# An mLSTM attention fused with a bilinear MLP: zero products ahead of the first transposes, a tile of their own for the gates, and another order of transfers and of the opening

## The chip, the cores and the metric

The kernel runs on one core of one Trainium2 chip. A core has the engines PE (TensorE, the matrix products), DVE (VectorE), ACT (ScalarE), POOL (GpSimd) and SP (SyncE, which here issues every DMA). The metric is device microseconds of one execution; lower is better. Before the change the median of three runs is 582.19 us (581.82 to 582.39).

## The reference, cut to what matters

For 4 batches and 8 heads a matrix memory C and a vector n run over 768 steps; the gated read-out y of all heads goes through a bilinear MLP. There is no softmax.

```python
for t in range(S):
    m_new  = np.maximum(f_gate[:, :, t] + m, i_gate[:, :, t])
    f_stab = np.exp(f_gate[:, :, t] + m - m_new)
    i_stab = np.exp(i_gate[:, :, t] - m_new)
    m = m_new
    C = f_stab * C + i_stab * einsum('bhd,bhe->bhde', vt, kt)
    n = f_stab * n + i_stab * kt
    h_tilde = einsum('bhde,bhe->bhd', C, qt)
    denom = np.maximum(np.abs(einsum('bhd,bhd->bh', n, qt)), 1.0)
    y[:, :, t] = sigmoid(o_gate[:, :, t]) * h_tilde / denom
x = y.transpose(0, 2, 1, 3).reshape(B * S, H * D)      # 3072 x 320
out = (x @ w_a) * (x @ w_b) @ w_out                    # 320 x 1536, 1536 x 320
```

The weights arrive in float64, everything else in float32.

## The kernel before, in words

**Attention.** The 768 steps are cut into 6 pieces of 128; a piece of one batch is a *chunk*, so there are 24, chunk n being piece n // 4 of batch n % 4. For a chunk the kernel transposes q and k on PE (`begin_a`, tile `pT`, copied to `T`), makes the table of decays (`begin_e`, product `pE` and an exponential into `gbc`), multiplies k by q (`pS`) and that by the table, multiplies by v (`begin_c`, `pV`), adds what the state of earlier pieces gives (`pI`), divides and gates it (`stage_f`, tiles `den`, `osig`), and turns it into the MLP's two operands `xh` and `xl` (`stage_d`, `pX`), a high and a low part. `weigh` makes `vw` = v times a column of weights on POOL; `stage_u` multiplies it by k into the state (`pU`, `cst`). From chunk 4 on the table comes from DRAM instead: the gates' sums are written to `g_dram`, `load_g` spreads them over 128 partitions into `gbc`, POOL masks them (line L405), and ACT takes eight exponentials (L412). From chunk 6 on q and k are split into three bf16 parts and turned by DMA transposes.

**MLP.** Nine *blocks* of 2 or 3 chunks go through `moe_block`. For each of 12 slices ff of the hidden width, `up(ff)` makes two sums `pu` of eight products each (the letter h or l of a weight is its high or low part), ACT copies the first, DVE multiplies by the second (`g`), and two slices later `down(ff)` adds three products per chunk into `pd`.

**Weights.** float64 cannot be computed with, so each piece of weights, a *stage* x from 0 to 31, is fetched raw (`fetch`) and converted by `high` (ACT), `low` and `join` (DVE, L347 and L352), `lead_part` (ACT, a copy that rounds, L365) and `low_part` (DVE, the rest, L371). Stages 0 to 4 serve slices 0 to 2 of the up-projection (0, 2 and 4 its first sum; 1, 3 and 4 its second), 5 to 7 the first three slices of the down-projection, 8 to 12 the next three slices up, and so on. `ready` tells how far the conversion stands, and `need` forces it.

**The order.** PE, ACT, DVE and SP work through fixed rows, in an order that a scheduler makes of the order of the code, of priorities and of `tc.issue_after`, which holds an instruction behind another one. What is written in the opening (after `manual_schedule`) is two chunks and stages 0 to 4 by hand. After it, `moe_block` yields after each product, and between products the generator `att` (the attention of later chunks) and `conv` (the weights) get their turns: `conv` at every sixth product.

**Rooms.** The gates' tables (`room`: f, i, m, `tab`, `gb`) sit in the slots s24 to s28, which are those of the raw weights of stages 24 to 28. So those can be fetched only when the gates are done, and `weights` fetches stage x + 16 as it converts stage x (`AHEAD`).

Of the kernel before, what the change touches and what calls it, by code (L numbers as in the profile page):

```python
# [8 lines left out]
F32 = mybir.dt.float32  # L9
BF16 = mybir.dt.bfloat16  # L10
# [10 lines left out]
def kernel(  # L21
# [116 lines left out]
    def load_qk(n, parts=(0, 1)):  # L138
        c, b = chunks[n]
        for j in parts:  # L140
            x = (q, k)[j]
            issued["qk"[j], n] = nc.sync.dma_start(  # L142
                nat(n)[0][:, j, :, 0:D], x[b, :, c * P:(c + 1) * P, :].rearrange("h t d -> t h d")
            ).ins

    def load_v(n):
        c, b = chunks[n]
        nc.sync.dma_start(
            nat(n)[1][:, :, 0:D], v[b, :, c * P:(c + 1) * P, :].rearrange("h t d -> t h d")
        )  # L150

    def load(n):
        load_qk(n)
        load_v(n)

    def fetch_o(c, b):
        if c not in osig:
# [25 lines left out]

        return x.bitcast(BF16).rearrange("p h (d w) -> p h d w", w=2)[:, :, :, 1]

    room = [rpool.tile([P, S], F32, tag=f"s{24 + j}", name=f"g_{n}") for j, n in enumerate(("f", "i", "m", "tab", "gb"))]
    gf, gi, gm = (x[0:BH] for x in room[0:3])
    tab = room[3][0:3 * BH].rearrange("p (c t) -> p c t", c=NC)
    gb3 = room[4][0:BH].rearrange("p (j w t) -> p j w t", j=3, w=2)

    def fetch_gates(cols):
        for t, x in ((gf, f_gate), (gi, i_gate)):
# [1 line left out]

    def first_gates():
        f, i, m = (x[:, 0:P] for x in (gf, gi, gm))
        g = gb3[:, 0]
        nc.vector.tensor_tensor_scan(m, f, i, -1e30, op0=ALU.add, op1=ALU.max)
        nc.vector.memset(f[:, 0:1], 0.0)
        nc.vector.tensor_tensor(f[:, 1:], f[:, 1:], m[:, 0:P - 1], op=ALU.add)  # L200
        nc.vector.tensor_tensor(f[:, 1:], f[:, 1:], m[:, 1:], op=ALU.subtract)
        nc.vector.tensor_tensor_scan(
            g[:, 0], one.broadcast_to([BH, P]), f, 0.0, op0=ALU.mult, op1=ALU.add
        )
        nc.vector.tensor_tensor(g[:, 1], i, m, op=ALU.subtract)
        nc.vector.tensor_tensor(g[:, 1], g[:, 1], g[:, 0], op=ALU.subtract)
        for j in range(3):
            x = gb3[:, j]
            (nc.scalar.copy if j < 2 else nc.vector.tensor_copy)(stk[j * BH:(j + 1) * BH], top(x))
            if j < 2:  # L210
                nc.vector.tensor_tensor(gb3[:, j + 1], x, top(x), op=ALU.subtract)

    def later_gates():
        f, i, m = (x[:, P:] for x in (gf, gi, gm))
# [6 lines left out]
        nc.vector.tensor_tensor(i, i, m, op=ALU.subtract)  # L221
        yield
        with tc.issue_after(start["act"]):
            nc.scalar.copy(G[:, 0], gb3[:, 0, 0])
            nc.scalar.copy(tab[BH:2 * BH, 0], gb3[:, 0, 1])
        for c in range(1, NC):
            nc.vector.tensor_tensor_scan(
                G[:, c], one.broadcast_to([BH, P]), gf[:, c * P:(c + 1) * P], 0.0,
# [78 lines left out]

    ready = [0]
    NF0 = 5
    AHEAD = 16  # L310

    def need(x):

# [355 lines left out]
    def moe_block(kb):  # L669
# [26 lines left out]
        def up(ff):  # L696
# [5 lines left out]
            for j in range(2):  # L702
                terms = []
                for kt in range(2):
                    h, l = w_up(ff, kt, j)
                    terms += [(h, xh[:, kt, :]), (h, xl[:, kt, :]), (l, xh[:, kt, :])]

                h = w_up(ff, 2, j)
                terms += [(h, xh[:, 2, :]), (h, xl[:, 2, :])]
                for x, (a, r) in enumerate(terms):  # L710
                    nc.tensor.matmul(  # L711
                        acc[j], a, r, start=(x == 0), stop=(x == len(terms) - 1),
                    )
                    yield
                if j == 0:
                    g = mpool.tile([P, NTB], F32, tag="acp", name=f"g{kb}_{ff}")[:, 0:NT]
                    (nc.vector.tensor_copy if kb > 0 and ff in [1, 2] else nc.scalar.copy)(g, acc[0])  # L717
# [35 lines left out]
    def begin_a(n):  # L753
# [6 lines left out]
        for j in range(2):  # L760
# [9 lines left out]
            for x in range(HH):  # L770
                after["t"] = nc.tensor.transpose(
                    pt[:, x], nat(n)[0][:, j, 2 * x:2 * x + 2, :].rearrange("t h d -> t (h d)"), ident
                ).ins
            (nc.vector.tensor_copy if n > 0 and j == 1 else nc.scalar.copy)(t, pt)
# [87 lines left out]
    with tc.manual_schedule(engines={mybir.EngineType[x] for x in ("PE", "Activation", "DVE", "SP")}):  # L862
        fetch_gates(slice(0, P))
        load_qk(0)
        fetch(0)
        load_qk(1)
        fetch(2)
        load_v(0)
        fetch(4)
        load_v(1)  # L870
        fetch_o(0, 0)
        fetch(1)
        fetch_o(0, 1)
# [19 lines left out]
        first_gates()  # L893
        run(A[0], 2)
        high(0)
        low(0)
        join(0)
        lead_part(0)
        run(E[0], 2)
        low_part(0)  # L900
        run(S_[0])
        run(A[1])
        high(2)
        low(2)
        join(2)
        run(S_[0])
        run(A[1])
        run(S_[0])
        run(E[1], 2)
        run(S_[1])  # L910
        lead_part(2)
        low_part(2)
        run(V[0], 2)
        squash(0, 0, 1)
        run(S_[1], 2)
        high(4)
        low(4)
        join(4)
        run(V[0])
        run(V[1], 2)  # L920
        run(F[0])
        lead_part(4)
# [89 lines left out]
```

## Time and profile before

| | before |
|---|---|
| median of three runs | 582.19 us |
| the profiled execution, its own time | 586.26 us |
| its span, first to last instruction | 584.5 us |
| PE busy | 543.7 us (93%) |
| DVE busy | 414.7 us (71%) |
| ACT busy | 220.0 us (38%) |
| POOL busy | 128.3 us (22%) |
| mean granted TensorE clock | 0.95 |

Busy time is the time in which an engine had at least one instruction under way. A row of the timeline has start and length in us, the engine (SPq is the issue of a DMA on SP), the line of the kernel, what is written from what, and in brackets how long the engine had been idle and what ended that. The granted clock is the share of the full TensorE clock that the chip's throttle allowed; the profile knows it from its first record, 8.9 us into the span, and shows 1.00 ahead of that.

### The profile page before, as it was taken

Reading aid. Unit: us, or ns where it says so; the run is one execution under the profiler, and the core shown is the slowest. Engines: PE = TensorE matmul, PEld = TensorE weight load, DVE = VectorE, ACT = ScalarE, POOL = GpSimd, SP = SyncE. Lnnn points to the kernel's source line nnn. Section 1 sums busy time; section 2 is a strip of 40 time slices with the busy share of each in tenths; the row PEclk is TensorE's granted clock in tenths of the full one; section 3 lists DMA queues with packets and bytes.
Section 4 is the critical chain, followed back from the end, with each engine's and each line's share of the span. In section 5 each row is a group of like instructions: output and inputs, shape, how many; then the busy total and the mean of one; then the engine's idle time right before and its main releaser. Section 6 shows DMA issues by size and latency. Waiting matters only on the chain.

```text
span 584.5 us, 12445 instructions
## 1 busy us (share of the span) xinstructions
PE 543.7 (93%) x4800; PEld 519.7 (89%) x4800; DVE 414.7 (71%) x947; ACT 220.0 (38%) x547; POOL 128.3 (22%) x181
## 2 busy tenths in 40 slices
PE   5697899999899989999799998998999999999997
PEld 5585799999799889999799898898999999999997
DVE  5689976457879767788739877678949774954332
ACT  5375854444323623323613323344413621411101
POOL 2002424444413230332103330312303201100000
PEclk9587669989999989999899999999999999999999
DMA  9995913494866774467634677566625832500000
GB/s 174 296 297 138 199 32 89 87 165 86 154 146 116 135 150 89 110 148 114 139 88 93 148 151 119 126 117 136 133 72 121 152 43 71 75 2 24 0 1 34
DMA packets 198678, 66.75 MB, mean 114 GB/s; under 512 B 184252, under 2 KB 191900, under 8 KB 198620
## 3 DMA queue, kind: packets, MB, share of 16 engines
q1 hardware_dynamic: 198620, 65.98, 54.3%
q8 instruction: 37, 0.61, 0.5%
q14 instruction: 21, 0.17, 0.1%
HBM read 41.11 MB, written 5.97 MB: 81 GB/s over the span
## 4 chain that ended last, share of the span: by engine, by line
PE 57%; DMA 13%; DVE 12%; SPq 9%; ACT 4%; issue 3%; POOL 0%; ACTq 0%; DVEq 0%
PE pu L711 32%; PE pd L684 14%; DMA T<-qks 4%; SPq L329 3%; PE pV L519 2%; DMA raw<-in_moe_w_out_dram 2%; DMA gbc<-g_dram 2%; DMA osig<-in_o_gate_dram 2%; SPq L159 2%; DVE gbc L472 2%; PE pX L618 2%; PE pV L836 1%; DMA c_dram<-cb 1%; SPq L142 1%; PE pS L784 1%
## 5 line engine op out<-in xcount | busy, mean ns | idle before, releaser
L711 PE MATMUL pu<-xh,w 128*128 128x384 f32 (+1 forms) x1080 | 285.0, 332 | 5.5 <-ACT g L717 1.5
L711 PE MATMUL pu<-xl,w 128*128 128x384 f32 (+1 forms) x648 | 211.5, 328 | 0.0
L711 PEld LDWEIGHTS pu<-xh,w 128*128 128x128 f32 x1080 | 197.5, 196 | 10.2 <-ACT g L717 2.8
L684 PE MATMUL pd<-w,gh 128*128 128x320 f32 x576 | 131.2, 315 | 2.0 <-ACT gh L720 1.6
L711 PEld LDWEIGHTS pu<-xl,w 128*128 128x128 f32 x648 | 126.5, 196 | 0.3
L718 DVE TENSOR_TENSOR g<-pu,g 128x384 f32<-128x384 f32 (+1 forms) x108 | 54.7, 507 | 76.9 <-PE pu L711 38.0
L684 PEld LDWEIGHTS pd<-w,gh 128*128 128x128 f32 x576 | 98.2, 191 | 3.0 <-ACT gh L720 2.1
L684 PE MATMUL pd<-w,gl 128*128 128x320 f32 x288 | 88.2, 316 | 0.1
L717 ACT COPY g<-pu 128x384 f32<-128x384 f32 (+1 forms) x92 | 40.3, 438 | 87.8 <-PE pu L711 77.2
L454 POOL TENSOR_TENSOR vr<-va 128x336 f32<-128x336 f32 x18 | 14.0, 779 | 212.7 <-PE pV L519 212.7
L684 PEld LDWEIGHTS pd<-w,gl 128*128 128x128 f32 x288 | 54.0, 190 | 0.9 <-DVE gl L722 0.3
L412 ACT ACTIVATE gbc<-gbc,gtab 128x128 f32<-128x128 f32 x160 | 49.3, 389 | 11.9 <-POOL gbc L405 9.6
L722 DVE TENSOR_TENSOR gl<-g,gh 128x384 fp32r<-128x384 f32 (+1 forms) x92 | 51.9, 564 | 1.9
L430 ACT CAST qks<-qk 128x320 bf16<-128x320 f32 x36 | 16.5, 457 | 80.4 <-DMA T<-qks 65.6
L720 DVE CAST gh<-g 128x384 fp32r<-128x384 f32 (+1 forms) x96 | 37.5, 390 | 1.6
L441 DVE COPY qks<-qks 128x320 bf16<-128x320 bf16 x36 | 10.4, 293 | 32.9 <-ACT qks L430 29.1
L405 POOL TENSOR_SCALAR_AFFINE_SELECT gbc<-gbc 128x1024 f32<-128x1024 f32 x20 | 25.5, 1277 | 21.1 <-DMA gbc<-g_dram 21.1
L595 POOL TENSOR_TENSOR osig<-osig,den 128x320 f32<-128x320 f32 x22 | 18.0, 819 | 48.9 <-DVE den L590 37.5
L519 PE MATMUL pV<-va,pb 128*128 128x42 bf16 x288 | 25.0, 182 | 0.6 <-DVE pb L478 0.6
L722 POOL TENSOR_TENSOR gl<-g,gh 128x256 fp32r<-128x256 f32 x16 | 13.0, 811 | 57.0 <-ACT gh L720 54.0
L519 PEld LDWEIGHTS <-pb 128*128 128x128 bf16 x576 | 23.0, 96 | 2.7 <-issue 0.9
L476 DVE TENSOR_TENSOR gbc<-gbc,pb 128x512 f32<-128x512 f32 x36 | 24.1, 683 | 1.0 <-ACT pb L474 0.8
(125 smaller groups left out, 807.3 us busy)
## 6 DMA issues: line engine op xcount, KB each, us to landing
gbc<-g_dram SPq DMA_DIRECT2D x20, 512.0 KB
qk<-in_q_dram SPq DMA_DIRECT2D x24, 160.0 KB
qk<-in_k_dram SPq DMA_DIRECT2D x24, 160.0 KB
va<-in_v_dram SPq DMA_DIRECT2D x24, 160.0 KB
osig<-in_o_gate_dram SPq DMA_DIRECT2D x24, 160.0 KB
raw<-in_moe_w_out_dram SPq DMA_DIRECT2D x12, 320.0 KB
out_dram<-o SPq DMA_DIRECT2D x24, 160.0 KB
raw<-in_moe_w_a_dram SPq DMA_DIRECT2D x8, 384.0 KB
```

The source lines that it names most:

```text
L329: raw_in = nc.sync.dma_start(raw[r0:r0 + a.shape[0]], a).ins
L405: nc.gpsimd.affine_select(E, E, pattern=[[0, H], [1, P]], compare_op=ALU.is_ge, fill=-1e30, base=0, channel_multiplier=-1,)
L412: nc.scalar.activation(E[:, h], E[:, h], AF.Exp, bias=beta[:, h:h + 1])
L476: nc.vector.tensor_tensor(E, E, pb[:, 0], op=ALU.subtract)
L519: nc.tensor.matmul(pv[:, h], pb[i][:, h % HH, :], vb[j][:, h], start=(x == 0), stop=(x == len(terms) - 1),)
L595: (nc.vector if n < NS else nc.gpsimd).tensor_tensor(yv, yv, den.unsqueeze(2).broadcast_to([P, H, D]), op=ALU.mult)
L684: nc.tensor.matmul(pd[t][:, 0:DM], a[:, cols], w, start=(ff == 0 and first), stop=(ff == NF - 1 and last),)
L711: nc.tensor.matmul(acc[j], a, r, start=(x == 0), stop=(x == len(terms) - 1),)
L717: (nc.vector.tensor_copy if kb > 0 and ff in [1, 2] else nc.scalar.copy)(g, acc[0])
L718: nc.vector.tensor_tensor(g, acc[1], g, op=ALU.mult)
L720: (nc.vector.tensor_copy if kb > 0 else nc.scalar.copy)(gh, g)
L722: (nc.gpsimd if kb * 12 + ff < 16 else nc.vector).tensor_tensor(gl, g, gh.bitcast(F32), op=ALU.subtract)
```

## The change

- Ten products of a zeroed tile (`idle`) go to a bank of their own (`warm`) at the head of PE's rows.
- The gates get tiles of their own (`gfim`, `g_tab`, `g_b`). So all stages are fetched in one run at the opening, `AHEAD` is gone, and the loads of chunk 3 and later, the write of `g_dram` and the first loads of `gbc` are held behind the last of the weights (`issued["w"]`).
- The attention's generator is held behind the first product of the first up-projection (`start["pe"]`), and so are chunk 2's transposes.
- The load of chunk 3 moves behind the state update of chunk 0, the long scan of the gates ahead of chunk 2's transposes, v of chunks 0 and 1 ahead by a stage, the second transposed copy of chunk 0 from ACT to DVE; the opening is written in another order; the conversion gets its turn at every fourth product of the first block.

```diff
     def load(n):
-        load_qk(n)
-        load_v(n)
+        with tc.issue_after(issued.get(("v", n - 1), issued["w"])):
+            load_qk(n)
+            load_v(n)
...
-    room = [rpool.tile([P, S], F32, tag=f"s{24 + j}", name=f"g_{n}") for j, n in enumerate(("f", "i", "m", "tab", "gb"))]
...
+    gfim = wpool.tile([3 * BH, S], F32, name="gfim")
+    gf, gi, gm = (gfim[j * BH:(j + 1) * BH] for j in range(3))
+    tab = wpool.tile([3 * BH, NC, P], F32, name="g_tab")
+    gbt = wpool.tile([3 * BH, 2, P], F32, name="g_b")
...
-        nc.sync.dma_start(g_dram.rearrange("c g t -> g c t"), G)
+        with tc.issue_after(issued["w"]):
+            nc.sync.dma_start(g_dram.rearrange("c g t -> g c t"), G)
...
     def weights():
         for x in range(NF0, len(stages) + 1):
-            fetch(x + AHEAD)
...
         for n in range(NS, NCH):
             if n + 1 < NCH:
-                with tc.issue_after(issued["w"]):
-                    load(n + 1)
+                if n > NS:
+                    with tc.issue_after(issued["w"]):
+                        load(n + 1)
...
-            (nc.vector.tensor_copy if n > 0 and j == 1 else nc.scalar.copy)(t, pt)
+            (nc.vector.tensor_copy if j == 1 else nc.scalar.copy)(t, pt)
...
-        for x in range(16, NF0 + AHEAD):
+        for x in range(16, 24):
             fetch(x)
+        for x in range(24, len(stages)):
+            fetch(x)
+
+        idle = apool.tile([P, H * DV], F32, tag="vr", name="idle").bitcast(BF16)[:, 0:512]
+        nc.vector.memset(idle, 0.0)
+        warm = ps_dn.tile([P, 512], F32, tag="pd2", name="warm")
+        for _ in range(WARM):
+            nc.tensor.matmul(warm, idle[:, 0:P], idle, start=True, stop=True)
...
     def rest():
+        gates = later_gates()
+        for _ in range(2):
+            next(gates)
+            yield
         yield from begin_a(NS)
         yield from begin_e(NS)
-        yield from later_gates()
+        yield from gates
         for n in range(NS):
             weigh(n)
             yield from stage_u(n)
+            if n == 0:
+                with tc.issue_after(issued["w"]):
+                    load(NS + 1)
...
-            if x % 6 == 0:
+            if x % (4 if kb == 0 else 6) == 0:
                 next(conv, None)
...
-                r = next(att, ("done", 99))
+                with tc.issue_after(start["act"]), tc.issue_after(start["dve"]), tc.issue_after(start["pe"]):
+                    r = next(att, ("done", 99))
```

Three places of the new order matter below. First ACT, from the second cast of `xh` (chunk 1, the last of the opening's attention) into the conversion. Before:

```order
L622 CAST xh_376<-pX_394 128x3x128
L365 CAST w_402<-cw 128x384
L340 ACTIVATE qks_90<-raw_168 128x384
L774 COPY T_0_427<-pT_0_428 128x512
L365 CAST w_409<-cw 128x384
L340 ACTIVATE qks_90<-raw_173 128x320
```

And now, where `w_443` is stage 3 as `w_409` was, and `T_0` is chunk 2's transposed q:

```order
L624 CAST xh_407<-pX_425 128x3x128
L368 CAST w_436<-cw 128x384
L343 ACTIVATE qks_90<-raw_166 128x384
L368 CAST w_443<-cw 128x384
L343 ACTIVATE qks_90<-raw_171 128x320
L343 ACTIVATE qks_89<-raw_173 128x320
L343 ACTIVATE qks_90<-raw_175 128x320
L343 ACTIVATE qks_89<-raw_177 128x384
L721 COPY g_0_471<-pu_0_0_449 128x256
```

The copy of chunk 2's q stood ahead of the cast of stage 3 and of all later stages; it now stands eleven rows behind that cast, and behind the first results of the up-projection.

Second SP's queue where the weights end. `qk_80` and `va_86` are the slots of chunk 0 that chunk 3 takes, `qk_81` that of chunk 4, and `gbc` the table of chunk 4. Before:

```order
L233 DMA g_dram<-g_tab 32x6x128
L329 DMA raw_540<-in_moe_w_a_dram 128x384
L179 DMA gbc_688<-g_dram 128x1024
L329 DMA raw_582<-in_moe_w_b_dram 128x384
L329 DMA raw_635<-in_moe_w_a_dram 128x384
L329 DMA raw_644<-in_moe_w_b_dram 128x384
```

And now:

```order
L332 DMA raw_231<-in_moe_w_out_dram 128x320
L142 DMA qk_80<-in_q_dram 128x8x40
L236 DMA g_dram<-g_tab 32x6x128
L148 DMA va_86<-in_v_dram 128x8x40
L142 DMA qk_81<-in_q_dram 128x8x40
L180 DMA gbc_697<-g_dram 128x1024
L142 DMA qk_80<-in_k_dram 128x8x40
```

The load of `gbc` went from the middle of the weights to a place behind v of chunk 3, whose slot is free only when POOL has made `vw` of chunk 0.

Third POOL, where `vw_597` and `vw_635` are chunk 0's and `vw_621` and `vw_662` chunk 1's. Before:

```order
L722 TENSOR_TENSOR gl_2_612<-g_2_572,gh_2_610 128x256
L405 AFFINE_SELECT gbc_688<-gbc_688 128x1024
L722 TENSOR_TENSOR gl_3_767<-g_3_727,gh_3_765 128x256
L820 TENSOR_TENSOR vw_597<-va_86,gtab 128x336
L820 TENSOR_TENSOR vw_621<-va_87,gtab 128x336
```

And now:

```order
L726 TENSOR_TENSOR gl_2_650<-g_2_609,gh_2_648 128x256
L824 TENSOR_TENSOR vw_635<-va_86,gtab 128x336
L726 TENSOR_TENSOR gl_3_781<-g_3_740,gh_3_779 128x256
L407 AFFINE_SELECT gbc_697<-gbc_697 128x1024
L824 TENSOR_TENSOR vw_662<-va_87,gtab 128x336
```

The mask of chunk 4's table moved from ahead of both `vw` to between them.

More of the change, by code (lines that the diff above doesn't have):

```diff
@@ L147, in load_v @@
         c, b = chunks[n]
-        nc.sync.dma_start(
+        issued["v", n] = nc.sync.dma_start(
             nat(n)[1][:, :, 0:D], v[b, :, c * P:(c + 1) * P, :].rearrange("h t d -> t h d")
-        )
+        ).ins
     def load(n):
-        load_qk(n)
-        load_v(n)
+        with tc.issue_after(issued.get(("v", n - 1), issued["w"])):
+            load_qk(n)
+            load_v(n)
     def fetch_o(c, b):
@@ L184, in top @@
         return x.bitcast(BF16).rearrange("p h (d w) -> p h d w", w=2)[:, :, :, 1]
-    room = [rpool.tile([P, S], F32, tag=f"s{24 + j}", name=f"g_{n}") for j, n in enumerate(("f", "i", "m", "tab", "gb"))]
-    gf, gi, gm = (x[0:BH] for x in room[0:3])
-    tab = room[3][0:3 * BH].rearrange("p (c t) -> p c t", c=NC)
-    gb3 = room[4][0:BH].rearrange("p (j w t) -> p j w t", j=3, w=2)
+    gfim = wpool.tile([3 * BH, S], F32, name="gfim")
+    gf, gi, gm = (gfim[j * BH:(j + 1) * BH] for j in range(3))
+    tab = wpool.tile([3 * BH, NC, P], F32, name="g_tab")
+    gbt = wpool.tile([3 * BH, 2, P], F32, name="g_b")
+    gb3 = [gbt[j * BH:(j + 1) * BH] for j in range(3)]
     def fetch_gates(cols):
@@ L196, in first_gates @@
         f, i, m = (x[:, 0:P] for x in (gf, gi, gm))
-        g = gb3[:, 0]
+        g = gb3[0]
         nc.vector.tensor_tensor_scan(m, f, i, -1e30, op0=ALU.add, op1=ALU.max)
@@ L207, in first_gates @@
         for j in range(3):
-            x = gb3[:, j]
+            x = gb3[j]
             (nc.scalar.copy if j < 2 else nc.vector.tensor_copy)(stk[j * BH:(j + 1) * BH], top(x))
             if j < 2:
-                nc.vector.tensor_tensor(gb3[:, j + 1], x, top(x), op=ALU.subtract)
+                nc.vector.tensor_tensor(gb3[j + 1], x, top(x), op=ALU.subtract)
     def later_gates():
@@ L223, in later_gates @@
         with tc.issue_after(start["act"]):
-            nc.scalar.copy(G[:, 0], gb3[:, 0, 0])
-            nc.scalar.copy(tab[BH:2 * BH, 0], gb3[:, 0, 1])
+            nc.scalar.copy(G[:, 0], gb3[0][:, 0])
+            nc.scalar.copy(tab[BH:2 * BH, 0], gb3[0][:, 1])
         for c in range(1, NC):
@@ L309 @@
     NF0 = 5
-    AHEAD = 16
+    WARM = 10
     def need(x):
@@ L710, in up @@
                 for x, (a, r) in enumerate(terms):
-                    nc.tensor.matmul(
+                    up_in = nc.tensor.matmul(
                         acc[j], a, r, start=(x == 0), stop=(x == len(terms) - 1),
-                    )
+                    ).ins
+                    start.setdefault("pe", up_in)
                     yield
@@ L866 @@
         load_qk(1)
+        load_v(0)
         fetch(2)
-        load_v(0)
+        load_v(1)
         fetch(4)
-        load_v(1)
         fetch_o(0, 0)
@@ L895 @@
         high(0)
+        run(E[0], 2)
         low(0)
@@ L898 @@
         lead_part(0)
-        run(E[0], 2)
-        low_part(0)
         run(S_[0])
         run(A[1])
+        run(S_[0], 2)
+        run(A[1])
+        low_part(0)
+        run(E[1], 2)
+        run(S_[1])
         high(2)
@@ L905 @@
         join(2)
[L906 to L910, printed above, removed]
         lead_part(2)
-        low_part(2)
         run(V[0], 2)
@@ L915 @@
         run(S_[1], 2)
-        high(4)
-        low(4)
-        join(4)
+        low_part(2)
         run(V[0])
@@ L921 @@
         run(F[0])
+        high(4)
+        run(F[0])
+        low(4)
+        join(4)
+        run(X[0])
         lead_part(4)
-        run(F[0])
-        run(X[0])
         squash(0, 1, 1)
@@ L927 @@
         run(F[1])
-        high(1)
-        low_part(4)
         run(X[0])
@@ L932 @@
         run(X[1])
-        run(X[0], 2)
+        run(X[0])
+        low_part(4)
+        high(1)
+        run(X[1])
         low(1)
         join(1)
-        run(X[1])
         lead_part(1)
+        run(X[1], 2)
+        run(X[0])
+        low_part(1)
         high(3)
-        run(X[1], 2)
-        low_part(1)
         low(3)
@@ L960, in rest @@
         for n in range(max(NS, NE), NS + 2):
-            load_g(n)
+            with tc.issue_after(issued["w"]):
+                load_g(n)
         yield from attention()
```

## The prediction, made before the changed kernel had run

> **What bounds the kernel now.** I read the page's clock line first, then busy time by stretch, then the waits of the first 150 us.
>
> ```profile
> span 584.5 us, 12445 instructions
> PEclk9587669989999989999899999999999999999999
> ...
> core 0: us, PE busy (x) PEld busy (x) DVE busy (x) ACT busy (x) POOL busy (x), PEclk, DMA share, GB/s
> 8.90:15.70 6.80, 5.45 (x70) 4.78 (x69) 3.93 (x8) 5.71 (x11) 0.00 (x0) 1.00 1.17 235
> 15.70:32.80 17.10, 11.67 (x54) 10.93 (x55) 10.34 (x27) 6.56 (x17) 0.00 (x0) 0.50 1.05 292
> 32.80:49.90 17.10, 12.91 (x118) 11.44 (x116) 17.04 (x34) 11.09 (x27) 2.97 (x4) 1.00 0.85 237
> 49.90:63.50 13.60, 12.61 (x52) 10.27 (x53) 13.34 (x29) 11.10 (x31) 3.30 (x3) 0.50 0.69 200
> 63.50:66.90 3.40, 1.85 (x24) 1.35 (x24) 3.40 (x10) 3.06 (x8) 2.26 (x1) 1.00 1.29 199
> 66.90:84.00 17.10, 16.16 (x94) 15.15 (x94) 13.75 (x30) 9.05 (x24) 4.97 (x8) 0.50 0.58 68
> 128.40:584.40 456.00, 434.66 (x4014) 420.63 (x4012) 322.73 (x739) 148.29 (x377) 91.75 (x115) 0.99 0.50 100
> ...
> PE pT L771 <- DMA qk<-in_q_dram: 8.5, 3, 4.9
> POOL gbc L405 <- DMA gbc<-g_dram: 12.5, 4, 5.5
> ```
>
> From 128 us on PE is busy for 434.66 of 456 us at a clock of 0.99: PE is the bound, and what reaches it earlier ends earlier. All that can be moved lies ahead of 84 us. There PE idles or runs at half clock (three stretches, 47.8 us), and from 32.8 to 63.5 us DVE is the bound, busy for 30.38 of 30.7 us: PE waits for weights that DVE is converting. So I follow DVE to stage 12, then PE.
>
> **The zero products.** PE's first work and the spacing of the `pE` products:
>
> ```profile
> 4.90 1.96 PE L771 MATMUL pT<-ident,qk 128*128 128x128 f32 x8 [4.90 <-DMA qk<-in_q_dram]
> 6.65 0.31 PE L747 MATMUL pE<-cx 96*128 96x128 bf16 x1
> 6.76 0.31 PE L748 MATMUL pE<-cx 96*128 96x128 bf16 x1
> ...
> 11.88 0.22 PE L747 MATMUL pE<-cx 96*128 96x128 bf16 x1
> 11.93 0.22 PE L748 MATMUL pE<-cx 96*128 96x128 bf16 x1
> ```
>
> Starts are 0.107 us apart at first and 0.057 us from 8.9 us on. A product of 512 columns, four times as wide, should take 4 x 0.107 = 0.43 us; ten take 4.3 us. After DVE's memset, an estimated start at 1.2 us ends them at 5.5 us, 0.6 us behind the landing of q (4.90). If they raise the clock in time, the 24 `pE` products of chunk 0 save 24 x 0.05 = 1.2 us. I take 0 for the sum, with -1.2 and +0.6 us as ends. The memset itself is ahead of `place`, which waits for POOL anyway; without that cover it would cost a fraction of a microsecond.
>
> **Chunk 2 behind the first up-projection.** PE, ACT and DVE around it:
>
> ```profile
> 15.59 6.96 PE L836 MATMUL pV<-va,gbc 128*128 128x42 f32 x32
> 29.52 1.09 PE L771 MATMUL pT<-ident,qk 128*128 128x128 f32 x4 [3.09 <-DMA qk<-in_q_dram]
> ...
> 30.64 0.59 ACT L774 COPY T<-pT 128x512 f32<-128x512 f32 x1 [2.84 <-PE pT L771]
> ...
> 31.67 0.56 DVE L371 TENSOR_TENSOR w<-cw,w 128x384 fp32r<-128x384 f32 x1 [2.74 <-ACT w L365]
> 32.15 0.56 DVE L347 TENSOR_SCALAR cw<-raw 128x320 uint32<-128x320 uint32 x2
> ...
> 97.56 1.72 PE pV L836 x16
> ```
>
> q of chunk 2 lands at 29.5 us. PE waits 3.09 us for it, ACT's copy stands behind PE, the cast of stage 3 behind that copy, and DVE idles 2.74 us. With the new order of ACT that cast waits for nothing of chunk 2, so DVE gains the 2.74 us. PE works meanwhile on 18 products of the up-projection, and the transposes that follow find q landed.
>
> The new opening also spreads chunk 0's two copies over ACT and DVE, gives `pE` of chunk 0 priority over the first weights and orders the rest otherwise. No row prices that. At best `pV` (6.96 us at half clock; 16 of its rows take 1.72 us at full clock, so 3.44 us for all) falls whole into a full-clock stretch: -3.5 us. At worst nothing. I take -1.4 us, nearer to nothing, since the opening's products are as sparse as before and the clock fell at 15.7 us. DVE thus reaches stage 5 at 32.15 - 2.74 - 1.4 = 28.0 us, 4.1 us earlier. Its list from there to the end of stage 12 is nearly the same by the order, and had no idle time to lose.
>
> **The gates' own tile and the late transfers.** Where that stretch ends:
>
> ```profile
> 52.98 1.91 DVE L371 TENSOR_TENSOR w<-cw,w 64x384 fp32r<-64x384 f32 x2
> ...
> 13.78 1.28 ACT L166 ACT_TABLE_LOAD   x1
> 54.47 0.37 ACT L717 COPY g<-pu 128x256 f32<-128x256 f32 x1 [1.97 <-POOL gbc L405]
> 55.32 2.45 ACT L412 ACTIVATE gbc<-gbc,gtab 128x128 f32<-128x128 f32 x8 [0.47 <-DVE gtab L256]
> 60.40 0.47 ACT L261 ACTIVATE gtab<-gtab 128x320 f32<-128x320 f32 x1
> ...
> 60.94 0.97 POOL L820 TENSOR_TENSOR vw<-va,gtab 128x336 f32<-128x336 f32 x1 [0.26 <-ACT gtab L261]
> 103.15 1.09 POOL L405 TENSOR_SCALAR_AFFINE_SELECT gbc<-gbc 128x1024 f32<-128x1024 f32 x1 [2.43 <-DMA gbc<-g_dram]
> ...
> 99.31 0.35 SPq L179 DMA_DIRECT2D gbc<-g_dram  x1
> 99.70 0.42 SPq L148 DMA_DIRECT2D va<-in_v_dram  x1
> ...
> 68.55 1.09 PE L543 MATMUL pU<-vw,qk 128*64 128x42 f32 x16
> 70.58 1.12 PE L771 MATMUL pT<-ident,qk 128*128 128x128 f32 x4 [0.94 <-DMA qk<-in_k_dram]
> 71.48 3.48 PE L836 MATMUL pV<-va,gbc 128*128 128x42 f32 x16
> 81.10 0.58 PE L711 MATMUL pu<-xh,w 128*128 128x256 f32 x1
> ```
>
> Stage 12 ends at 52.98 + 1.91 = 54.9 us before, so at 50.8 us now. Before, ACT's exponential of `gtab` (60.40) stood behind the eight of `gbc` and the casts and copies between; now it stands behind the first copy of slice 3 and a table load, the price of a sigmoid that moved between two exponentials. Give the last product 0.5 us; then 50.8 + 0.5 + 0.37 + 1.28 + 0.47 + 0.97 puts the end of chunk 0's `vw` at 54.4 us, against 61.9. A second added table load lies on ACT during conversion, where ACT is busy for 11.09 of 17.10 us; without that slack it would cost 1.3 us.
>
> Here the new wait sits. SP issues v of chunk 3 (0.42 us) only after that `vw`, then q (0.42), then `gbc`. The row at 99.31 took until 103.15 to reach POOL, 3.84 us; then the mask 1.09 and the second `vw` 0.97. So `pU` of chunk 1 starts at 54.4 + 0.9 + 3.84 + 1.09 + 0.97 = 61.2 us. PE and ACT's exponentials wait for it, some 4 us of PE, where before PE lost some 3 us on q, `g`, `vw` and k. Still it is 7.3 us ahead of the row at 68.55. PE is eight products further back there by the order (8 x 0.21 at half clock = 1.7 us) and needs no wait for k (0.94): 6.6 us ahead at the row 71.48, and so at 81.10.
>
> The weights of stages 24 to 31 come earlier, which by itself I cost at nothing: DVE's row never waits for them before. The conversion's denser turns I also cost at nothing, since DVE is full.
>
> **Sum.** -2.7 - 1.4 on DVE, -3.4 more at `vw`, +0.9 from the new stall and the eight products: -6.6 us, carried to the end by a PE that is the bound. The profiled execution took 586.26 us; it would take 579.7. The median of the runs stands 4.07 us below it: 582.19 - 6.6 = 575.6 us.
>
> **The rivals.**
>
> *The clock comes back sooner* (chance 0.2). From 66.9 us the clock stays at half for 17.1 us although PE is busy for 16.16. Ahead of 81 us these are narrow products (`pV` of 42 columns, `pU`, `pS`), behind it wide ones, and it rises after 3 us of those. If the earlier and denser stretch gets full clock some 8 us sooner, that saves 4 us more: 571.6 us. [...]
>
> *The lead is lost later* (0.12). PE idles 21.3 us behind 128 us. If the chain from chunk to chunk sets the pace there and not PE, and the loads of chunks 4 and 5 that now come behind `vw` hold that chain where it was, the whole 6.6 us go: 582.2 us. Against it: the first links of that chain start earlier too.
>
> *The table of chunk 4 comes late* (0.08, the side of slower). It decides where the `gbc` load takes over 3.84 + 6.6 = 10.4 us; the slowest wait for one before was 5.5 us. Eight exponentials then block ACT, ACT's casts block DVE, and PE's idle time keeps the half clock for a stretch of 17.1 us more (8.5 us lost, less 6.6): 584 us.
>
> *The zero products do nothing but delay* (0.05). Then +0.6 us: 576.2 us. [...]
>
> **How the numbers follow.** The forecast, 573 to 579 us, has 0.55. The low end: DVE's shift at its best (another -3.3 us) and 2 us of clock give 570. The high end: only the 2.74 us on DVE (+1.4), a `gbc` of 5.5 us (+1.7) and one more half-clock stretch of 3.4 us (+1.7) give 580.4, and half of the lead lost later 581.5. The range is 569.5 to 581.5. A change under 0.2% (1.2 us) cannot be told from none here. Faster: the forecast, the clock, the zero products and some of the lost lead, 0.83; same, 0.08; slower, 0.09.
>
> **What would show it.** `pE` spaced 0.057 us from its first row; `pu` ahead of chunk 2's `pT`, with no 3 us of idle PE; DVE's 128x320 conversion at 28 us; `vw` of chunk 0 near 54 us; a wait of POOL for `gbc` right behind it, and PE idle ahead of `pU`. Wrong if the half-clock stretches grow, if ACT stands still ahead of the exponentials of chunk 4's table for over 8 us, or if PE idles more behind 128 us.

## The result, and the profile after

| | before | changed |
|---|---|---|
| median, 13 runs each | 583.45 us (581.29 to 587.42) | 578.71 us (575.57 to 581.17) |
| ratio, 95% interval | | 0.9915 (0.9889 to 0.9942): 5.0 us less, 3.4 to 6.5 |
| the same kernel once more, in a later group | 583.35 us | 578.16 us, 0.992 (0.9881 to 0.996) |
| profiled execution, its span | 586.26, 584.5 us | 578.71, 576.9 us |

The time of 575.6 us that was predicted is 3 us low, inside the range; the gain of 6.6 us was a little over the interval. The profiled execution of before lies 2.8 us above its own median, so the two traces differ by more (7.6 us) than the kernels do. Ratios, here and below, leave out executions more than 1.5% above the fastest of their kernel: one of 23 and one of 17 of before in two groups, one of six of the kernel with 21 more zero products, and three of six (576 us) of the last kernel in the table.

From the page of after and from its busy time by stretch, in the columns used before:

```profile
span 576.9 us, 12438 instructions
PEclk9577689998999899999899999999999999999999
...
8.90:15.70 6.80, 6.80 (x85) 6.44 (x81) 5.17 (x13) 4.88 (x9) 0.00 (x0) 0.98 1.11 250
15.70:32.80 17.10, 10.89 (x47) 9.56 (x48) 14.50 (x32) 10.29 (x25) 0.00 (x0) 0.50 1.01 259
32.80:49.90 17.10, 14.87 (x116) 12.56 (x115) 15.18 (x33) 12.08 (x26) 2.63 (x4) 0.90 1.05 325
49.90:63.50 13.60, 11.21 (x60) 9.44 (x60) 11.74 (x29) 9.34 (x22) 2.14 (x3) 0.51 0.84 189
66.90:84.00 17.10, 17.10 (x119) 16.05 (x119) 13.74 (x32) 11.83 (x33) 5.43 (x8) 0.71 0.37 63
128.40:576.80 448.40, 426.62 (x3949) 413.73 (x3947) 324.17 (x736) 147.50 (x373) 90.27 (x113) 0.99 0.52 102
```

DVE is no longer full between 32.8 and 63.5 us (26.92 of 30.7 us, before 30.38). The clock stays at half for one window longer at the front (up to 35.9 us, before 32.8) and comes back earlier, within the stretch of 66.9 to 84.0 (0.71, before 0.50). Where the gain sits shows in the first 90 us, before and then changed:

```profile
0.00:90.00 90.00, 70.64 (x485) 63.20 (x486) 70.87 (x157) 54.23 (x128) 19.55 (x40) 0.73 0.80 186
0.00:90.00 90.00, 75.84 (x545) 65.84 (x545) 74.07 (x164) 58.92 (x136) 19.51 (x46) 0.75 0.77 188
```

PE idles 14.2 us there, before 19.4; from 90 to 540 us it idles 18.1, before 17.6. So the gain is idle time of PE that went ahead of 90 us, as the prediction had it. It is hardly the clock: the mean granted clock is 0.957 over the 13 executions, and 0.956 over 57 of before from the groups below (the clock's record begins 3.8 us earlier in the changed kernel's trace, and what that start is worth is not in these means).

Now the places that the prediction named, from the timelines of PE, DVE, ACT, POOL and SP:

```profile
1.19 4.27 PE L896 MATMUL warm<-idle 128*128 128x512 bf16 x10 [1.19 <-DVE idle L893]
7.00 0.22 PE L751 MATMUL pE<-cx 96*128 96x128 bf16 x1
7.06 0.22 PE L752 MATMUL pE<-cx 96*128 96x128 bf16 x1
...
20.75 0.88 PE L620 MATMUL pX<-ident,osig 128*128 128x128 f32 x3 [2.06 <-DVE osig L600]
30.56 1.09 PE L775 MATMUL pT<-ident,qk 128*128 128x128 f32 x4 [2.58 <-DMA qk<-in_q_dram]
...
26.38 0.32 DVE L350 TENSOR_SCALAR cw<-raw 128x320 uint32<-128x320 uint32 x1
26.74 1.54 DVE L219 TENSOR_TENSOR_SCAN gfim<-gfim 32x640 f32<-32x640 f32 x1
50.60 0.56 DVE L374 TENSOR_TENSOR w<-cw,w 64x384 fp32r<-64x384 f32 x1
52.84 0.47 ACT L264 ACTIVATE gtab<-gtab 128x320 f32<-128x320 f32 x1
53.39 0.75 POOL L824 TENSOR_TENSOR vw<-va,gtab 128x336 f32<-128x336 f32 x1 [8.12 <-ACT gtab L264]
...
54.22 0.38 SPq L148 DMA_DIRECT2D va<-in_v_dram  x1
55.16 2.86 SPq L142 DMA_DIRECT2D qk<-in_q_dram  x1
59.02 0.34 SPq L180 DMA_DIRECT2D gbc<-g_dram  x1
63.09 1.09 POOL L407 TENSOR_SCALAR_AFFINE_SELECT gbc<-gbc 128x1024 f32<-128x1024 f32 x1 [6.80 <-DMA gbc<-g_dram]
65.02 0.67 PE L545 MATMUL pU<-vw,qk 128*64 128x42 f32 x16 [1.67 <-POOL vw L824]
66.11 3.04 PE L840 MATMUL pV<-va,gbc 128*128 128x42 f32 x16
```

Up to `vw` the chain falls where it was put: stage 12 ends at 51.2 us (50.8 predicted), `vw` of chunk 0 at 54.14 (54.4). The second `pX` comes 4.8 us earlier than before (25.55). But PE still waits 2.58 us for q of chunk 2, and behind `vw` the table comes 4 us later than predicted.

### The profile page after: what moved, and what is told of

Its sections match the earlier page's. It is cut to its first block, busy times and chain, and to the rows that moved or that the text cites. A ratio compares the mean times of both kernels' runs of the same rounds, so it can differ in the third digit from the quotient of the medians.

```text
span 576.9 us, 12438 instructions
## 1 busy us (share of the span) xinstructions
PE 540.9 (94%) x4810; PEld 515.9 (89%) x4810; DVE 418.5 (73%) x949; ACT 222.5 (39%) x548; POOL 127.4 (22%) x181
## 4 chain that ended last, share of the span: by engine, by line
PE 57%; DVE 12%; DMA 10%; issue 4%; SPq 3%; ACT 2%; POOL 0%; ACTq 0%; DVEq 0%; POOLq 0%
PE pu L714 33%; PE pd L687 14%; DMA T<-qks 7%; PE pV L521 2%; DVE gbc L474 2%; PE pX L620 2%; DVE r L436 1%; SPq L446 1%; SPq L160 1%; DMA gbc<-g_dram 1%; PE pU L545 1%; DVE qks L437 1%; PE pS L469 1%; PE pV L840 1%; DVE gh L724 1%
## 5 line engine op out<-in xcount | busy, mean ns | idle before, releaser
L726 DVE TENSOR_TENSOR gl<-g,gh 128x384 fp32r<-128x384 f32 (+1 forms) x92 | 53.2, 578 | 1.9
L443 DVE COPY qks<-qks 128x320 bf16<-128x320 bf16 x36 | 11.9, 334 | 38.4 <-ACT qks L432 31.9
L407 POOL TENSOR_SCALAR_AFFINE_SELECT gbc<-gbc 128x1024 f32<-128x1024 f32 x20 | 25.2, 1261 | 14.3 <-DMA gbc<-g_dram 12.4
L597 POOL TENSOR_TENSOR osig<-osig,den 128x320 f32<-128x320 f32 x22 | 17.6, 800 | 47.5 <-DVE den L592 36.6
L521 PE MATMUL pV<-va,pb 128*128 128x42 bf16 x288 | 25.1, 182 | 0.6 <-DVE pb L480 0.6
L602 ACT COPY osig<-osig 128x64 f32<-128x64 f32 x24 | 5.9, 245 | 50.0 <-DVE osig L600 50.0
```

The source lines that it names most:

```text
L407: nc.gpsimd.affine_select(E, E, pattern=[[0, H], [1, P]], compare_op=ALU.is_ge, fill=-1e30, base=0, channel_multiplier=-1,)
L521: nc.tensor.matmul(pv[:, h], pb[i][:, h % HH, :], vb[j][:, h], start=(x == 0), stop=(x == len(terms) - 1),)
L597: (nc.vector if n < NS else nc.gpsimd).tensor_tensor(yv, yv, den.unsqueeze(2).broadcast_to([P, H, D]), op=ALU.mult)
L726: (nc.gpsimd if kb * 12 + ff < 16 else nc.vector).tensor_tensor(gl, g, gh.bitcast(F32), op=ALU.subtract)
```

## Experiments

The rows behind the opening are put in order by a scheduler that reckons with times of its own, so each edit below also moves some rows of the free part. The table gives the ratio to before; from each one's profiled execution PE's busy time (page, first part), the number of windows of 3.41 us that the clock spent at half (up to 540 us, from the clock's own record; in brackets those behind 90 us), PE's idle time from 90 to 540 us, the start of the first `pX` product of chunk 1, and two leads in us. A lead is how much earlier than in the trace of before PE starts a certain product: the 488th (in before at 90.3 us; zeros are not counted, and each kernel has 4800 others), and the first `pX` of chunk 23, the last chunk (in before at 521.4 us). `pX` of chunk 2 would not do as a mark: in before it stands behind 174 products of the MLP, in the changed kernel behind 142. Gains in us below are the ratio times the median of before (583.2 to 583.7 in the groups); leads are against the one profiled execution of before, which was 2.8 us slow, so they flatter by about that. The clock's record begins between 3.9 us (both of the last two) and 16.1 us (opening alone); half clock ahead of that is not in the count.

| kernel | ratio (95%) | PE busy | half windows | PE idle, 90 to 540 us | chunk 1 | lead, product 488 | lead, chunk 23 |
|---|---|---|---|---|---|---|---|
| before | 1 | 543.7 | 17 (3) | 17.6 | 25.6 | 0 | 0 |
| changed | 0.9915 (0.9889 to 0.9942) | 540.9 | 16 (3) | 18.1 | 20.8 | 5.7 | 7.6 |
| zero products alone | 0.9852 (0.9811 to 0.9894) | 537.3 | 13 (2) | 13.6 | 23.9 | 3.1 | 9.9 |
| opening alone | 0.9895 (0.9847 to 0.9942) | 535.6 | 10 (1) | 17.6 | 25.1 | 6.4 | 10.0 |
| gates' tile and late transfers alone | 0.9908 (0.9874 to 0.9941) | 535.3 | 11 (0) | 13.5 | 24.1 | 1.0 | 10.9 |
| chunk 2 behind alone | 1.0035 (1.0005 to 1.0065) | 541.7 | 15 (3) | 17.6 | 26.0 | 1.1 | 1.1 |
| changed, no zero products | 0.9965 (0.9929 to 1.0002) | 543.6 | 18 (3) | 15.6 | 22.2 | 2.1 | 4.7 |
| changed, table first | 0.9961 (0.9933 to 0.9989) | 540.7 | 15 (3) | 19.4 | 20.5 | 5.4 | 5.3 |
| changed, chunk 2 ahead | 0.9846 (0.9786 to 0.9905) | 539.2 | 14 (2) | 15.9 | 20.5 | 3.8 | 8.4 |
| changed, q of chunk 2 early | 0.9796 (0.9754 to 0.9838) | 536.7 | 13 (2) | 14.7 | 20.5 | 6.4 | 13.5 |
| changed, 21 more zero products | 0.9786 (0.973 to 0.9842) | 535.8 | 7 (1) | 15.4 | 20.9 | 7.6 | 14.6 |
| both of the last two | 0.9735 (0.9694 to 0.9775) | 532.8 | 5 (0) | 15.6 | 20.8 | 11.5 | 19.4 |
| both, and chunk 2 ahead | 0.9719 (0.9672 to 0.9767) | 531.5 | 5 (0) | 17.1 | 21.0 | 12.4 | 19.2 |

**The four parts, each alone on the kernel before.** The zero products:

```diff
+        for _ in range(WARM):
+            nc.tensor.matmul(warm, idle[:, 0:P], idle, start=True, stop=True)
```

> The kernel before with the ten zero products alone. Theory (they help in the opening and the rest takes it back): the clock rises near 5 us, the pE of chunk 0 are spaced 0.057 us from the first, the first pX comes 0.5 to 1.5 us earlier than 22.34, and the ratio is 0.997 to 1.001. Rival (they carry some 3 us, as the changed kernel without them suggests): 0.993 to 0.996.

The opening is as the theory had it (first `pX` at 20.70 us, 1.6 earlier), the time is not: 8.6 us less, more than either expected. At product 488 this execution is 3.1 us ahead, at the end 9.9. DVE even waits longer behind q of chunk 2 than before (2.74 us there):

```profile
32.90 0.56 DVE L372 TENSOR_TENSOR w<-cw,w 128x384 fp32r<-128x384 f32 x1 [5.62 <-ACT w L366]
```

So most of the gain is not the one that the products make in the opening; it arises behind 90 us, where PE idles 4.0 us less than before and one half-clock window is gone. What in the edit does that, the products or the rows that the scheduler moved, this run does not tell.

The opening (order of its rows and transfers, and the copy on DVE):

```diff
-            (nc.vector.tensor_copy if n > 0 and j == 1 else nc.scalar.copy)(t, pt)
+            (nc.vector.tensor_copy if j == 1 else nc.scalar.copy)(t, pt)
```

> The kernel before with the new opening alone: the order of its rows, of its transfers, and the second copy of chunk 0 on DVE. Theory (it brings the first up-projection 3 us forward, and the wait for q of chunk 2 and the half clock take most of it back): first pX near 19 us, PE's wait for q of chunk 2 longer than 3.1 us, ratio 0.996 to 1.000. Rival (the opening carries the gain of the change): 0.995 or less.

6 us less, the rival's side. The first `pX` stayed at 22.33 us, where the theory wanted 19: without the zero products the clock rose at 16.1 us in this execution. The gates' tile with the late transfers:

```diff
-    room = [rpool.tile([P, S], F32, tag=f"s{24 + j}", name=f"g_{n}") ...
+    gfim = wpool.tile([3 * BH, S], F32, name="gfim")
...
+        for x in range(24, len(stages)):
+            fetch(x)
```

> The kernel before with the gates in tiles of their own, all stages of weights fetched in one run at the opening, and the later transfers behind them; no zero products, the old opening, chunk 2 where it was. Theory (costed at nothing by the prediction): 0.998 to 1.002. Rival A (the earlier weights carry the gain of the change): 0.994 or less. Rival B (loads of chunks 3 to 5 come late, and the chain from chunk to chunk is behind at 120 us): 1.003 or more, with waits of PE for T<-qks between 90 and 160 us.

5.4 us less: rival A. At product 488 it is 1.0 us ahead, at the end 10.9; PE is busy for 70.00 us of 70.00 between 90 and 160 us, and no half-clock window is left behind 90. This trace shows the kernel at its best: the clock of 0.967 is the highest of its 12 executions (mean 0.959). And holding chunk 2 back:

```diff
-                r = next(att, ("done", 99))
+                with tc.issue_after(start["act"]), tc.issue_after(start["dve"]), tc.issue_after(start["pe"]):
+                    r = next(att, ("done", 99))
```

> The kernel before with one part of the change: the attention behind the first product of the up-projection, and the scan of the gates ahead of chunk 2's transposes. Theory (the prediction's term: DVE gains the 2.74 us that it waited behind q of chunk 2): DVE's wait near 31 us goes, vw of chunk 0 comes 2 to 3 us earlier, the ratio is 0.993 to 0.996. Rival (what DVE gains there it loses to other waits or to the clock, as the faster run with chunk 2 ahead suggests): 0.998 to 1.004.

The rival: 2 us more. DVE's and ACT's timelines there show why:

```profile
30.43 0.32 DVE L347 TENSOR_SCALAR cw<-raw 128x320 uint32<-128x320 uint32 x1
30.66 1.53 DVE L217 TENSOR_TENSOR_SCAN g_m<-g_f,g_m,g_i 32x640 f32<-32x640 f32 x1
...
36.18 0.47 ACT L166 ACTIVATE osig<-osig 128x320 f32<-128x320 f32 x1 [2.56 <-DMA osig<-in_o_gate_dram]
39.66 1.09 ACT L751 ACTIVATE gbc<-pE 128x512 f32<-128x512 f32 x2
40.63 0.46 ACT L365 CAST w<-cw 128x320 fp32r<-128x320 f32 x1
41.12 0.49 DVE L371 TENSOR_TENSOR w<-cw,w 128x320 fp32r<-128x320 f32 x1 [2.64 <-ACT w L365]
```

DVE's 2.74 us near 31 us are gone, and it waits 2.64 us at 41: the next cast stands on ACT behind the exponentials of the same chunk 2, which came later.

The conversion's denser turns in the first block belong to none of these four parts, and no run has them alone.

**Parts taken out of the changed kernel.** Without the zero products:

```diff
-    WARM = 10
+    WARM = 0
```

> The changed kernel with WARM = 0; the opening's order is the same, the free part that follows is re-ordered by the scheduler in 20 or so rows of each engine. Theory (the gain is idle time of PE between 18 and 70 us that the new order removes, the zero products bring nothing): the clock rises about 4 us after the first pT, near 9 us, pE of chunk 0 is spaced 0.107 us, the first pX comes 0 to 1 us later than in the changed kernel (17.80), and the time stays at 0.9915 of before within 0.003. Rival (the earlier clock carries the gain): the first pX comes 3 us or more later and the ratio is 0.997 or more.

2.9 us are lost against the changed kernel, near the rival's bound, but the interval takes in both. The first `pX` comes 1.2 us later. ACT's rows of the free part changed too, with nine table loads up to 130 us instead of seven, so this run alone does not price the products. Then the stall that the prediction put behind `vw`:

```diff
             if NE <= n + 2 < NCH:
-                load_g(n + 2)
+                table = load_g(n + 2)
+                if n == NS:
+                    with tc.issue_after(table):
+                        load_v(NS + 1)
...
-                    load(NS + 1)
+                    load_qk(NS + 1)
```

> The changed kernel with the load of chunk 4's table ahead of v of chunk 3 and q of chunk 4 on SP, so that it no longer stands behind a transfer that waits for POOL. Theory (the new wait of gbc, POOL, vw, pU cost what the prediction undersized): POOL's wait of 6.8 us for gbc and PE's 1.7 us ahead of the second pU go, pU of chunk 1 starts at 61 to 62 us instead of 65.0, and the ratio falls by 0.003 to 0.005, to about 0.987. Rival (the wait is paid back by the clock, whose windows decide, or by later waits): pU earlier but the ratio at 0.9915 within 0.002.

Neither: the second `pU` came 2.0 us earlier, and the kernel was, if anything, slower than the changed one (0.9961, with intervals that overlap). PE in this kernel, and two of the clock's windows; behind them the two windows of the changed kernel in that place:

```profile
62.98 0.94 PE L545 MATMUL pU<-vw,qk 128*64 128x42 f32 x16 [3.46 <-POOL vw L827]
65.98 3.48 PE L843 MATMUL pV<-va,gbc 128*128 128x42 f32 x16
...
59.79:63.20 3.41, 0.22 (x8) 0.22 (x8) 3.41 (x7) 1.41 (x6) 2.02 (x2) 1.00 1.08 159
63.20:66.61 3.41, 2.26 (x24) 2.11 (x20) 0.47 (x2) 3.36 (x10) 0.75 (x1) 0.50 0.84 138
```

```profile
59.75:63.17 3.42, 3.42 (x27) 3.25 (x26) 1.94 (x5) 1.59 (x4) 0.08 (x1) 0.50 0.82 198
63.17:66.58 3.41, 1.74 (x27) 1.51 (x26) 2.11 (x4) 2.31 (x7) 2.54 (x3) 1.00 0.18 27
```

The wait was longer but earlier: nearly all of it lay in the window up to 63.2 us, and the next ran at half clock. In the changed kernel the window up to 63.17 us was full of work. `pV` starts 0.1 us apart in the two, and the lead is gone. The edit did not take the stall away either: POOL still waited 5.03 us for the table. What SP waited for before it issued the table's load, in this kernel and then in the changed one (total, times, longest):

```profile
SPq L180 <- DMA g_dram<-g_tab: 5.3, 1, 5.3
SPq L180 <- DMA g_dram<-g_tab: 0.9, 1, 0.9
```

The load reads what the write of `g_dram` brings, and the change holds that write behind the last of the weights: SP issued it at 50.67 us here and at 52.45 in the changed kernel, and went on with the load at 57.10 and 59.02; before, 45.6 and 47.5. In the changed kernel, too, this was the wait that ended last. Last, chunk 2 ahead again:

```diff
-        gates = later_gates()
-        for _ in range(2):
-            next(gates)
-            yield
         yield from begin_a(NS)
         yield from begin_e(NS)
-        yield from gates
+        yield from later_gates()
...
-                with tc.issue_after(start["act"]), tc.issue_after(start["dve"]), tc.issue_after(start["pe"]):
+                with tc.issue_after(start["act"]), tc.issue_after(start["dve"]):
```

> The changed kernel with chunk 2's transposes free to go ahead of the first up-projection again, and ahead of the scan of the gates, as before the change; the scheduler also puts the load of gbc ahead of v of chunk 3. Theory (DVE's 2.74 us behind q of chunk 2 was a main term): DVE waits 2 to 3 us near 30 us again, the weights come that much later, and the ratio is 0.995 to 0.997. Rival (PE waits for q of chunk 2 in the changed kernel too, 2.58 us, so that the move bought nothing): ratio 0.9915 or below.

Some 4 us less than the changed kernel, on the rival's side, with intervals that overlap: of the four parts this is the one that seems to cost, here as alone. The scheduler also put the table's load first here, which by the run before is no gain.

**The clock and q of chunk 2.** More zero products between the halves of `pV` and behind both `pX`, 21 in all:

```diff
-        run(V[0], 2)
+        run(V[0])
+        zeros(3)
+        run(V[0])
+        zeros(3)
...
         run(X[0])
+        zeros(5)
```

> The changed kernel with 21 more zero products between the halves of pV and behind both pX, where PE runs narrow products or waits. Theory A (the clock falls at 15.4 us because narrow products and waits count as idle): the clock stays full beyond 15.4 us, to 22 us or further; the added products cost 21 x 0.21 = 4.5 us of PE, much of it in waits; the opening's pV takes 3.4 us instead of 5.0, and the ratio is 0.988 to 0.993. Theory B (the clock falls for another reason than what PE does): half clock from 15.4 us as before, the added products cost 21 x 0.43 = 9 us of which some 4 lie in waits, and the ratio is 0.998 to 1.003.

Theory A, and more than it asked: 0.9786. Three of the clock's windows over `pV` in the changed kernel, then in this one:

```profile
8.56:11.97 3.41, 3.41 (x50) 3.17 (x50) 2.63 (x5) 2.23 (x5) 0.00 (x0) 1.00 1.10 241
11.97:15.38 3.41, 3.41 (x39) 3.29 (x37) 2.63 (x7) 2.68 (x5) 0.00 (x0) 1.00 1.14 251
15.38:18.79 3.41, 3.31 (x16) 2.90 (x15) 2.77 (x10) 2.06 (x6) 0.00 (x0) 0.50 1.10 263
```

```profile
14.36:17.77 3.41, 3.41 (x28) 2.86 (x27) 2.83 (x9) 2.15 (x4) 0.00 (x0) 1.00 1.09 294
17.77:21.18 3.41, 2.96 (x20) 1.75 (x20) 2.31 (x7) 2.24 (x6) 0.00 (x0) 1.00 0.97 300
28.02:31.43 3.41, 0.85 (x6) 0.69 (x6) 1.59 (x5) 0.62 (x3) 0.00 (x0) 1.00 1.03 124
31.43:34.84 3.41, 3.33 (x24) 3.19 (x24) 2.13 (x3) 2.60 (x5) 0.00 (x0) 0.50 0.99 290
```

The window 11.97 to 15.38 held 16 `pS` (40 rows) and 21 `pV` (42 columns); PE was busy throughout, and yet the next ran at half clock. In the kernel with q early, whose run follows, such a window holds hardly anything but `pV`:

```profile
12.76:16.17 3.41, 3.41 (x33) 3.41 (x31) 3.07 (x8) 2.76 (x5) 0.00 (x0) 1.00 1.23 255
16.17:19.58 3.41, 1.45 (x7) 0.92 (x6) 2.13 (x8) 2.05 (x6) 0.00 (x0) 0.50 1.03 283
```

With wide zero products among them the clock stayed at 1.00 up to 31.43 us; in the window that ends there PE, which waited 4.3 us for q of chunk 2, was busy for 0.85 us, and the next one ran at 0.50. Whether the 42 columns, the f32 type or something else in `pV` stands behind the falls at 15.38 and 16.17 us, no run separates. The wait for q was taken next, by fetching it earlier:

```diff
-        for x in range(5, 13):
+        for x in range(5, 8):
             fetch(x)
-        load(2)
+        load_qk(2)
+        for x in range(8, 13):
+            fetch(x)
+        load_v(2)
```

> The changed kernel with q and k of chunk 2 fetched ahead of the weight stages 8 to 12 instead of behind them. Both theories: q lands near 25 us instead of 30.5 and PE's 2.6 us ahead of chunk 2's pT go. Theory (idle time of PE ahead of 84 us is carried to the end): 2 to 3 us less than the changed kernel, a ratio of about 0.987. Rival (DVE sets the pace up to 60 us, and the windows of the clock round the rest): within 1 us of the changed kernel, 0.990 to 0.993.

The theory's direction at more than twice its size: 6.3 us less than the changed kernel in the same group. q is there at 23.9 us, 6.6 us earlier:

```profile
23.93 1.09 PE L775 MATMUL pT<-ident,qk 128*128 128x128 f32 x4 [1.44 <-DMA qk<-in_q_dram]
```

Yet `pX` of chunk 2 is only 0.4 us ahead of the changed kernel's in its second run (80.1), the last `pX` 4.4 us (512.2). Both edits together:

> The 21 further zero products of the run before together with q and k of chunk 2 ahead of stages 8 to 12. Theory (the clock fell at 31.4 us there because PE stood still for 4.3 us ahead of it): the clock stays full to 45 us or further, and the ratio goes from 0.979 to 0.972 to 0.976. Rival (DVE is the bound up to 60 us, a faster PE only waits longer): the clock stays full, and the ratio stays at 0.979 within 0.003.

And with the edit that puts chunk 2 ahead again, as above:

> The kernel with 31 zero products in the opening and q and k of chunk 2 ahead of stages 8 to 12, and now chunk 2 free to go ahead of the up-projection again, and ahead of the scan of the gates. Theory (holding chunk 2 back costs some 2 us, as it did alone on the kernel before): a ratio of 0.968 to 0.972. Rival (with q early and the clock full the place of chunk 2 does not matter): 0.9735 within 0.003.

The first came to 0.9735, as the theory had it, though the clock stayed full to 38.1 us and not to 45. The second came to 0.9719, on three executions: with q early and the clock up, the place of chunk 2 makes no difference that shows. These two are the fastest of the case, some 16 us under before. The changed kernel itself, unedited, was run beside the runs with q early and with chunk 2 behind alone:

> The changed kernel itself once more, as the measure for the others of this group on their chip. Every theory: 0.9915 of before within 0.003.

It was at 0.992.

The granted clock of every execution is on record, so what these edits gain can be set against it. One minus the clock, times the span, is an estimate of the time that half clock takes, if PE has work throughout. It is 24.9 us on average in the 13 executions of the changed kernel and 25.7 in its eight of the later group; 12.4 with the 21 zero products, 19.8 with q early, 10.8 with both. The differences to the changed kernel, less an estimated 4.5 us for the added products where there are any (21 at 0.21 us; in the trace with the 21, three take 0.66 us, from 15.24 to the next `pV` at 15.90), are 8.0, 5.8 and 10.4 us; the times fell by 7.5, 7.2 and 10.8. By this estimate the clock accounts, within a microsecond or two, for what these three gain over the changed kernel.

## Why the prediction was right, and where it was not

**Right in sign and in kind, and nearly in size by errors that cancel.** The kind is the one forecast: idle time of PE ahead of 84 us went, and the lead was carried to the end. That the sum of 6.6 us came so near to 5.0 is luck in good part, as its steps show:

- *The zero products, 0, between -1.2 and +0.6.* They ended at 5.46 us (5.5 predicted), and `pE` is spaced 0.06 us from its first row. The bounds were the step that failed: alone they give 8.6 us, and taking them out of the change costs 2.9. I had bounded them by the rows that they speed up, and left out that whatever shifts the rows behind them also changes PE's waits there and where these fall in the clock's windows (alone, behind 90 us: 13.6 us idle, before 17.6, and two half-clock windows, before three).
- *Chunk 2 behind the up-projection, -2.74 on DVE.* The wait went, as said, but the sum stopped there. "The transposes that follow find q landed" failed: PE came earlier too and waited 2.58 us, because q's load stood behind stages 8 to 12 (30.56 against 23.93 us with the load moved). Alone, this part makes the kernel slower by 2 us.
- *The new opening, -1.4, at best -3.5.* Mis-sized: the second `pX` came 4.8 us earlier. That is a gain of the opening and the zero products together: alone the one brings 0.4 us there, the other 1.6.
- *`vw` at 54.4 us.* 54.14. DVE reached stage 5 at 26.4 us, 1.6 earlier than said, and then took the gates' scan of 1.54 us ahead of the rest of it; from there on the terms held.
- *The stall on the table.* Found, but mis-sized, with a wait left out. SP's issue of q of chunk 4 took 2.86 us and not 0.42 (the trace of before has one of 4.29 us, for v of chunk 2 at 23.56), but behind it SP still waited 0.9 us for the write of `g_dram`, which the prediction's chain does not contain. A short issue alone would not have helped: with the table first, nothing of the kind stood ahead of the load, and yet the write took as long from its issue to the load's (6.4 us, here 6.6; before, 1.9). `pU` came at 65.02 instead of 61.2.
- *The earlier weights, at nothing.* Alone, the gates' tile with the late transfers gives 5.4 us, nearly all of it behind 90 us. The reason given was that DVE never waits for these weights; it does not cover what else the later transfers and the new order change.
- *The clock.* The first rival happened in its stretch (its 8 us were an estimate that no row of before shows): back at full from 76.8 us, 7.2 us sooner, an estimated 3.6 us of work. But the half clock at the front was one window longer, which takes back up to 1.7, so it paid for about half of the stall's 3.8 us.
- *Carried to the end by a PE that is the bound.* For the change itself it held: 5.7 us ahead at product 488, 7.6 at the end. No kernel of the table loses its lead behind 90 us. But some gain as much there again or more: the gates' tile goes from 1.0 to 10.9 us ahead, the zero products from 3.1 to 9.9, while table first stays where it was (5.4 and 5.3). PE's time behind 90 us is not fixed: PE's waits there, and the half-clock windows that follow them, differ from order to order (13.5 to 19.4 us idle and none to three such windows in the table), and a sum that ends at 81 us cannot see that.

**The windows.** This lies behind the last point: in each of the twelve other rows of the table, what a kernel gains behind 90 us equals, within 2.5 us, the idle time of PE that it saves there plus 1.7 us for each half-clock window that it has less. All changes of the clock in one trace are multiples of 3.41 us apart (before, up to 84 us: 8.90, 15.72, 32.79, 49.86, 63.51, 66.92, 83.99; changed: 5.14, 15.38, 35.86, 49.52, 63.17, 66.58, 76.82). I cut all 14 traces (before, changed, and the twelve) into these windows: of the full-clock windows in which PE idled 1.6 us or more, 40 of 41 were followed by one at half clock; of those with less than 0.8 us idle, 12 of some 1800, nine of them in the opening's `pS` and `pV`; between the two, 16 of some 136. Two windows of the changed kernel behind 100 us and their successors, and one that just stayed:

```profile
128.02:131.44 3.42, 1.59 (x17) 1.27 (x16) 0.85 (x4) 0.92 (x2) 0.00 (x0) 1.00 1.05 254
131.44:134.85 3.41, 3.41 (x21) 3.32 (x20) 3.38 (x9) 0.66 (x2) 2.75 (x4) 0.50 1.11 185
192.88:196.29 3.41, 1.46 (x10) 1.30 (x10) 3.41 (x9) 1.77 (x3) 1.00 (x2) 1.00 0.32 43
196.29:199.70 3.41, 3.03 (x25) 3.02 (x25) 2.69 (x7) 3.41 (x11) 0.00 (x0) 0.50 0.27 71
390.84:394.26 3.42, 1.91 (x26) 1.58 (x25) 3.42 (x10) 2.58 (x9) 0.51 (x1) 1.00 0.10 24
394.26:397.67 3.41, 3.41 (x23) 3.41 (x22) 3.38 (x8) 1.79 (x5) 0.00 (x0) 1.00 0.82 169
```

With 1.59 and 1.46 us of work in 3.41 the next window ran at half, with 1.91 it did not. A half-clock window full of work costs an estimated 1.7 us (half of 3.41) beside the wait in the window ahead of it. The kernels with 14 recorded windows or fewer are those at a ratio of 0.991 or less, those with 15 to 18 at 0.9915 or more, and PE's busy time falls nearly in the order of that column. With the half clock ahead of the record estimated as well (its start over 3.41 us: 8.90 us, 2.6 windows, in before), the three parts that gain alone come to about 15 each and before to 20. This is a correlation over single executions, not an experiment on one cause; the experiment is the one with 21 more zero products. The windows do not begin with PE's first product: in the nine traces that begin with the ten zero products, always at 1.19 us, the clock first rises between 3.94 and 6.53 us.

**What stays open.** Three parts each gain 5 to 9 us alone, their sum would be 20, and the whole gains 5. The part on chunk 2 explains some 2 to 4 of the difference. How much of the rest is that each part removes the same half-clock windows, and how much the scheduler's other order behind the opening, no run here separates (nor what the conversion's denser turns do): the zero products, for one, could not be taken out without moving other rows.

## What to carry to other kernels

Before pricing a wait of PE, ask in which window of the clock it falls and what the next window holds: here 1.7 us of idle PE in a window of 3.41 could cost an estimated 3.4, itself and 1.7 in the next window (at half clock in 40 of 41 cases from 1.6 us up), and 1.3 us mostly just itself (16 of some 136 between 0.8 and 1.6), so that removing half of a wait can be worth more or less than its length. Where PE waited or ran narrow products early in this kernel, 21 wide products of zeros brought 7.5 us: try them, and time the whole kernel, not the stretch. And a transfer that PE will wait for is moved in the queue before the work around it is re-ordered: q ahead of five stages of weights brought 6.3 us, about as much as the whole change. Ahead of such a move, follow the wait to what ends last: the table's load did not gain by going first, since the write that it reads had not landed (SP waited 5.3 us for it).

## What the runs showed of the hardware that was not expected

- The clock rose behind products of zeros as it did behind others: in before at 8.90 us, 4.0 behind the first product, a transpose of q; in the changed kernel at 5.14 us, 3.95 behind the first of the ten (2.75 to 5.34 in the nine traces that begin so) and ahead of any other product (the first `pT` starts at 5.29).
- PE busy for 3.41 of 3.41 us, nearly all of it with f32 products of 42 columns, was followed by a window at 0.50 (rows 12.76:16.17 and 16.17:19.58); with wide zero products in between, three behind each eight, the clock stayed at 1.00 (rows 14.36:17.77 and 17.77:21.18).
- SP's issue of one 160 KB load took 0.42 us in one place (99.70 us, before) and 2.86 in another of the same kind (55.16 us, changed); the length of an issue row is not a constant.
